# Two stacked experts behind attention: one d_ff group of the first out matrix by seven block products, and a new plan

## The chip, the core and the metric

One core of one Trainium2 chip runs the whole program as one launch. The metric is the device time in microseconds (us), as the median of several executions. The engines are TensorE (PE), VectorE (DVE), ScalarE (ACT), GpSimd (POOL) and SyncE (SP, which issues most DMAs). Each engine works through its own instructions in the order in which they stand in the program, and semaphores order the engines against each other.

## What is computed

```python
# attention: 4 batches, 12 heads, 448 tokens, head width 64; q and k are RMS-normed first
attn_out = softmax(scale * q_n @ k_n.T) @ v
x = attn_out.transpose(0, 2, 1, 3).reshape(1792, 768)
# first expert: d_model 768, d_ff 2048
h = x @ w_in
g = np.where(h > 0.0, h, np.exp(np.minimum(h, 0.0)) - 1.0)
x = g @ w_out
# second expert: d_ff 1536
xn = x / rms * rms_g
g = xn @ w_gate
out = (g * sigmoid(g) * (xn @ w_val)) @ w_out2
```

## The kernel before

Activations lie transposed: d_model or d_ff on the 128 partitions, the 448 tokens of one batch along the row. All products are fp32. An operand is split into a high part, rounded to the type that TensorE takes at full pace, and a low part, the remainder; a 128x128 weight tile times 448 columns is then three matmuls (`mm3`, line 1159: high·high, high·low, low·high). A split is a copy (`copy`, on DVE, ACT or POOL) and a subtraction (`tt`, on DVE or POOL).

The work runs in stages (`STAGES`, line 617): attention for batch 0 alone, then the first expert for batch 0, for batch 1, the second expert for batches 0 and 1, the first expert for batches 2 and 3, the second expert for batches 2 and 3. Attention for the later batches is spread between them. In the stages with two batches a block of 2x2 matrices is multiplied with seven products instead of eight (`quad`, line 1193): the weights enter as A11, A12, A22 and four combinations S1 to S4, the activations as B11, B21, B22 and four combinations T1 to T4 made by `combo` (line 1220). Each combination is split like any operand. In `combo` the first combination, `t1 = b12 - b11` (line 1233), has both inputs in SBUF; for the second product of an expert (`tx is GX`) it is written to a PSUM bank.

Batches 2 and 3 of the first expert ("stage 3" below, counting from 0) have d_ff in four groups of four tiles. Each group makes h by two `h_quad` calls (seven products each, 63 matmuls), and then adds its share of `g @ w_out` with `acc_units` (line 1341), eight plain products: 6 output tiles, 2 batches, 4 d_ff tiles, 3 matmuls, that is 144 matmuls. The last stage, the second expert for batches 2 and 3 ("stage 4"), has three groups, each four `quad`s for gate and value, two `combo`s over their results, and three `quad`s for the out matrix, all from weight blocks that were split earlier and stored in DRAM, and are loaded by DMAs on POOL's queue (`b_ahead`, line 682).

Weights arrive packed (`w_convert`), are kept as fp32 in DRAM (`kept`) where they are used again, and are split into a ring of four SBUF tiles (`r_w`), which gets a fifth when stage 3 begins (line 1558). Combinations of weights for stage 4 are made ahead of time by `job` (line 697) during stage 3.

No instruction is issued when the code above is run. Everything is recorded (`plan.add`), and `Plan` (line 33) lays the recorded operations onto the five engines by list scheduling with prices per operation: `forward` places operations by rank, `backward` makes new ranks from the result, and the best of several passes is kept. `issue` then emits the order; that is why all of it carries line 348. `Plan.add` marks an operation `shared` if none of its operands is in PSUM: such a DVE operation is priced as unable to run beside a GpSimd operation. At the start `issue` also fills PE's waits with idle matmuls on `small` into bank 130 (`idle`), whose number comes from planned start times.

## Time and profile before

| | |
|---|---|
| median of 3 runs | 1226.96 us (1224.61 to 1228.07) |
| the profiled execution: its own time | 1222.62 us |
| the profiled execution: span from first to last instruction | 1220.8 us |
| busy: PE, DVE, ACT, POOL | 99%, 75%, 58%, 68% of the span |
| mean granted TensorE clock | 0.997 of full speed |

The profile is one execution. The rows read from it name an engine, an operation, what it writes and reads (tile names without buffer numbers: `gbig`, `xs` and `late` are operands' halves, `w` split weights, `bank` PSUM), and in brackets the time for which the engine had been idle and what ended that. A tile called `late` is a buffer of the attention that is used again under another type.

### The profile page before, as it was taken

What the parts mean: (1) busy time and instruction counts of PE and PEld (TensorE: products, weight loads), DVE (VectorE), ACT (ScalarE), POOL (GpSimd) and SP (SyncE); (2) the same over time, 40 slices, a digit from 0 to 9 for tenths busy, and PEclk for the clock granted to TensorE, in tenths of its full rate; (3) what the DMA queues carried; (4) which work ended last, traced back from release to release, by engine and by line L of the source; (5) the groups of instructions that cost most, each with busy time, mean ns of one, the idle gap of its engine ahead of it and who ended that gap; (6) DMA issues with size and microseconds to landing.
All of it is one profiled execution on the core that took longest, in us unless ns stands there. A gap on an engine that the chain in (4) does not pass through costs nothing.

```text
span 1220.8 us, 18816 instructions
## 1 busy us (share of the span) xinstructions
PE 1204.1 (99%) x6296; PEld 1012.9 (83%) x6296; DVE 919.7 (75%) x1521; ACT 711.1 (58%) x1447; POOL 835.6 (68%) x721
## 2 busy tenths in 40 slices
PE   9899999999999999999999999999999999999998
PEld 7458777778777787778999999999999988988997
DVE  7777988899535579754799799947666799568678
ACT  6986877767665677765564564756444743221121
POOL 3467887888657485427897699866464978476573
PEclk9999999999999999999999999999999999999999
DMA  7677886885534458856599799756452275965766
GB/s 253 202 261 251 277 288 208 265 249 180 171 121 123 142 202 308 268 165 212 189 343 313 258 372 327 245 175 196 158 184 96 70 219 158 269 197 157 237 192 202
DMA packets 120164, 265.52 MB, mean 217 GB/s; under 512 B 15742, under 2 KB 59012, under 8 KB 120068
## 3 DMA queue, kind: packets, MB, share of 16 engines
q1 hardware_dynamic: 90260, 205.79, 50.1%
q0 software_dynamic: 21168, 49.55, 14.3%
q10 hardware_dynamic: 8640, 8.99, 2.9%
q8 instruction: 49, 0.80, 0.3%
q14 instruction: 47, 0.39, 0.1%
HBM read 183.11 MB, written 81.17 MB: 216 GB/s over the span
## 4 chain that ended last, share of the span: by engine, by line
PE 89%; DVE 7%; ACT 3%; issue 1%; ACTq 0%; DVEq 0%
PE bank L348 89%; DVE bank L348 2%; DVE tbig L348 1%; ACT p L348 1%; ACT tbig L348 1%; DVE gbig L348 0%; ACT pt L348 0%; DVE wc L348 0%; DVE wt L348 0%; DVE pt L348 0%; ACT tk L348 0%; DVE ybig L348 0%; DVE ss L348 0%; ACT ybig L348 0%; DVE pj L348 0%
## 5 line engine op out<-in xcount | busy, mean ns | idle before, releaser
L348 PE MATMUL bank<-xs,w 128*128 128x448 f32 x1731 | 401.3, 371 | 1.3 <-DVE late L348 0.8
L348 PE MATMUL bank<-gbig,w 128*128 128x448 f32 x1603 | 361.2, 370 | 0.2 <-DVE gbig L348 0.2
L348 PEld LDWEIGHTS bank<-xs,w 128*128 128x128 f32 x1731 | 317.7, 188 | 35.9 <-issue 8.5
L348 PEld LDWEIGHTS bank<-gbig,w 128*128 128x128 f32 x1603 | 296.5, 188 | 31.6 <-issue 6.6
L348 POOL TENSOR_TENSOR w<-wc,w 128x768 fp32r<-128x768 f32 (+1 forms) x106 | 195.4, 1846 | 51.9 <-ACT w L348 37.3
L348 PE MATMUL bank<-late,w 128*128 128x448 f32 x647 | 164.1, 367 | 2.7 <-ACT late L348 2.7
L348 DVE TENSOR_REDUCE bank<-bank 128x1 f32<-128x448 f32 x168 | 98.8, 624 | 53.7 <-PE bank L348 53.6
L348 PEld LDWEIGHTS bank<-late,w 128*128 128x128 f32 x647 | 121.8, 188 | 13.9 <-ACT late L348 3.5
L348 POOL TENSOR_SCALAR w<-wc 128x768 fp32r<-128x768 f32 (+1 forms) x50 | 46.1, 922 | 80.7 <-PE bank L348 71.8
L348 ACT ACTIVATE p<-bank,nm,rr 128x448 f32<-128x448 f32 x126 | 90.2, 720 | 18.4 <-DVE nm L348 16.2
L348 DVE SCALAR_TENSOR_TENSOR wc<-wc,wt 128x768 int32<-128x768 int32 x68 | 87.4, 1285 | 16.6 <-ACT wc L348 10.0
L348 ACT ACTIVATE tbig<-bank 128x448 f32<-128x448 f32 x85 | 46.0, 542 | 76.0 <-PE bank L348 54.5
L348 ACT ACTIVATE pt<-bank 128x384 f32<-128x384 f32 (+2 forms) x175 | 75.3, 451 | 24.2 <-PE bank L348 20.5
L348 ACT ACTIVATE w<-wc 128x768 fp32r<-128x768 f32 (+1 forms) x75 | 58.5, 782 | 42.7 <-PE bank L348 34.0
L348 DVE TENSOR_TENSOR ybig<-bank,ybig 128x448 f32<-128x448 f32 x72 | 44.4, 618 | 40.6 <-PE bank L348 40.3
L348 PE MATMUL bank<-ident,p 128*128 128x128 f32 x441 | 69.9, 277 | 2.3 <-ACT pt L348 2.2
L348 DVE TENSOR_TENSOR tbig<-bank,tbig 128x448 f32<-128x448 f32 x93 | 56.4, 618 | 20.6 <-PE bank L348 18.9
L348 DVE TENSOR_SCALAR wt<-wr 128x768 uint16<-128x768 uint16 x68 | 68.6, 1009 | 1.1 <-DMA wr<-wst 0.8
L348 PEld LDWEIGHTS bank<-ident,p 128*128 128x128 f32 x441 | 53.7, 141 | 17.5 <-ACT pt L348 5.4
L348 ACT ACTIVATE wt<-wr 128x768 uint16<-128x768 uint8 x50 | 54.4, 1089 | 22.7 <-DVE wc L348 12.2
L348 POOL TENSOR_TENSOR ql<-rw,qh 128x512 fp32r<-128x512 f32 x38 | 53.8, 1431 | 3.2 <-ACT qh L348 2.6
L348 PE MATMUL bank<-pt,rv 128*64 128x448 f32 x252 | 53.1, 550 | 1.0 <-ACT pt L348 1.0
(264 smaller groups left out, 2251.1 us busy)
## 6 DMA issues: line engine op xcount, KB each, us to landing
wr<-wst SPq DMA_DIRECT2D x68, 768.0 KB
wc<-kept SPq DMA_DIRECT2D x64, 384.0 KB
kept<-wc SPq DMA_DIRECT2D x52, 384.0 KB
w<-bgv_S POOLq DMA_DIRECT2D x38, 384.0 KB, 3.9
bgv_A<-w SPq DMA_DIRECT2D x36, 384.0 KB
bgv_S<-w SPq DMA_DIRECT2D x32, 384.0 KB
rw<-qk SPq DMA_DIRECT2D x21, 512.0 KB
w<-bgv_A POOLq DMA_DIRECT2D x28, 384.0 KB, 4.1
```

The costliest lines, as they stand in the source:

```text
L348: return lambda *a, **k: f(*[real(x) for x in a], **{n: real(x) for n, x in k.items()})
```

## The change

1. **Stage 3, group 1 by seven products.** The new function `fast_experts` takes the place of `first_experts` for batches 2 and 3. For d_ff group 1 (`SEVEN = (1,)`) the out matrix is no longer added by eight plain products but by three `quad`s, 3 x 7 x 2 x 3 = 126 matmuls for 144. The weights' blocks come from `w_out`, which reads them from `kept` and makes S1 to S4 with four `tt`; the activations' blocks come from a `combo` over the four h tiles of each `h_quad`. For this group the accumulators `ybig` go to DRAM (`parts`) and their space is lent to the operands; the sums of the group go through `parts` too, and are loaded back behind it.
2. **First halves ahead.** The first `h_quad` of a group now stands ahead of the out products of the group before it.
3. **Split out weights kept.** On their second use (batch 1) the split out weights of groups 0, 2 and 3 are stored in DRAM (`both`, 12 tiles of 768 KB), and stage 3 loads them by POOL's queue instead of splitting them.
4. **Blocks in pairs.** Stage 4's weight blocks are stored and loaded two to a DMA (`pairs`): 87 DMAs on POOL's queue in the whole program where there were 147. `job` makes gate and value blocks in halves.
5. **The fifth weight tile** joins only behind stage 3; its space holds h and partial sums during it.
6. **The plan.** Another seed, then 20 local changes of rank (`MOVES`); an operation with two inputs in SBUF and its output in PSUM now counts as `shared`; the number of idle matmuls comes from a second pass over the finished order (`times`).

```diff
-    PASSES = 12
-    SEED = 33
+    PASSES = 11
+    SEED = 47
+    MOVES = (
+        (645977, 260.9, 275.9, 8.0, 1, 0),
...
-        shared = port and not any(getattr(ap.tensor, "_space", None) == PSUM for ap in list(outs) + list(ins) if ap is not None)
+        banked = [getattr(ap.tensor, "_space", None) == PSUM for ap in list(outs) + list(ins) if ap is not None]
+        shared = port and not any(banked[len([o for o in outs if o is not None]):] if sum(not b for b in banked) > 1 else banked)
...
+        for seed, lo, hi, size, own, more in self.MOVES:
+            noise = random.Random(seed)
+            rank = list(best[1]) if own else self.backward(*best)
+            for i in range(n):
+                if lo <= best[1][i] < hi:
+                    rank[i] += size * (noise.random() - 0.5)
+            for _ in range(more):
+                rank = self.backward(*self.forward(rank))
+            best = self.forward(rank)
...
-        t, end = self.IDLE[0], self.start_t[self.first_use]
+        at = self.times(order, eng)
+        t, end = self.IDLE[0], at[self.first_use]
...
+    r_y = Ring(tiles=r_sq.t + [wr[0][:, k * S:(k + 1) * S] for k in range(2)])
...
+    r_h = Ring(tiles=[pt_own[0][:, k] for k in range(3)] + [wr[0][:, 2 * S:3 * S]])
...
+                res += ins(g, 1) + ins(g + 1, 0) if g else ins(0, 0) + ins(0, 1) + ins(1, 0)
+                if g in SEVEN:
+                    res += [("o", j, nums[k + nf], q) for q in range(3) for j in range(3)]
+                else:
+                    res += [("c", nums[k + nf + j]) for j in range(OG)]
...
+            if n in both:
+                w = spl_w[i] = r_w.next()
+                dma(w.rearrange("p a n -> p (a n)"), both[n].rearrange("p a n -> p (a n)"), P * WN * 8, by="g")
+                return
...
+    def w_out(i, j, n0, q):
+        n = 2 * P
+        if j == 0:
+            c, s0, s1 = r_wc.next(), r_ws.next(), r_ws.next()
+            a21 = s1[:, n:2 * n]
+            for x, v in ((a21, 4), (c[:, 2 * n:3 * n], 6), (c[:, 0:n], 0), (c[:, n:2 * n], 2)):
+                m, k = divmod(8 * q + v, CW)
+                dma(x, kept[n0 + m][:, k * P:k * P + n], P * n * 4)
...
+            tt(x1, a21, a22, ALU.add)
+            tt(x2, x1, a11, ALU.subtract)
+            tt(x3, a11, a21, ALU.subtract)
+            tt(s1[:, 0:n], a12, x2, ALU.subtract)
+            duo["o"] = (c, s0, s1[:, 0:n])
+        spl_w[i] = split_w(duo["o"][j], n if j == 2 else WN)
...
+    def spread_h(f, bs, hs, seven):
+        if not seven:
+            for (i, j), t in hs.items():
+                split_g((f + i, bs[j]), t)
+            return
+        combo(f // 2 % 2, [hs[i, j] for j in range(2) for i in range(2)], {}, GX, gslots, 2)
...
+            if first:
+                ahead = h_quad(f0, bs)
+                yield
+            spread_h(f0, bs, ahead, seven)
+            h = h_quad(f0 + 2, bs)
+            if last:
+                drop_combos()
+            spread_h(f0 + 2, bs, h, seven)
+            yield
+            if not last:
+                ahead = h_quad(f0 + NF1, bs)
+                yield
+            if not seven:
+                yield from acc_units(bs, f0, NF1, first, last, y, False, y_done)
+                continue
+            for k in range(3):
+                quad(out_eat(first, E_ORDER[2 * k:2 * k + 2]), tx=GX, take=take_out)
...
-                    r_w.grow([wide[0].rearrange("p (a n) -> p a n", a=2)])
                     combos(ahead[1])
...
+            r_w.grow([wide[0].rearrange("p (a n) -> p a n", a=2)])
             j = r_w.k % len(r_w.t)
-            r_b.t = [t.rearrange("p a n -> p (a n)")[:, h * WN:(h + 1) * WN] for t in r_w.t[j:] + r_w.t[:j] for h in range(2)]
+            r_b.t = [t.rearrange("p a n -> p (a n)") for t in r_w.t[j:] + r_w.t[:j]]
```

PE's queue at the start of the program, before and then after. The rows on `small` are the idle matmuls; `ident,rsb` makes the gain of the norms, `ident,rr` spreads the first norm factors that k waits for, `qh` and `ql` are the first scores.

```order
L348 MATMUL bank_130<-small 128x128 x28
L348 MATMUL bank_133<-ident,rsb_125 128x1
L348 MATMUL bank_130<-small 128x128 x20
L348 MATMUL bank_134<-ident,rr_114 64x128 x8
L348 MATMUL bank_130<-small 128x128 x3
L348 MATMUL bank_134<-ident,rr_114 64x128 x8
L348 MATMUL bank_130<-small 128x128 x3
L348 MATMUL bank_127<-qh 128x448
```

```order
L445 MATMUL bank_130<-small 128x128 x35
L445 MATMUL bank_133<-ident,rsb_125 128x1
L445 MATMUL bank_130<-small 128x128 x6
L445 MATMUL bank_134<-ident,rr_114 64x128 x8
L445 MATMUL bank_130<-small 128x128 x3
L445 MATMUL bank_134<-ident,rr_114 64x128 x8
L445 MATMUL bank_130<-small 128x128 x3
L445 MATMUL bank_127<-qh 128x448
```

Seven idle matmuls moved ahead of the gain, and fourteen of the twenty behind it are gone.

ACT's queue during the attention of batch 0, before and then after. `pe` and `pt` are copies of transposed probabilities out of the banks 131 to 133, which PE's next transposes write; `tk` squares tokens for a later norm; `p` and `tbig` with `sm` are exponentials.

```order
L348 ACTIVATE p_106,sm_117<-bank_127,nm_119,rr_114 128x448
L348 ACTIVATE pe_110<-bank_131 64x64 x2
L348 ACTIVATE tk_99<-tk_99 128x960
L348 ACTIVATE pt_107<-bank_131 128x3x64
L348 ACTIVATE pt_108<-bank_131 128x3x64
L348 ACTIVATE ybig<-bank_133 128x384
```

```order
L445 ACTIVATE pe_110<-bank_131 64x64 x2
L445 ACTIVATE pt_108<-bank_131 128x3x64
L445 ACTIVATE pt_107<-bank_131 128x3x64
L445 ACTIVATE p_106,sm_117<-bank_130,nm_119,rr_114 128x448
L445 ACTIVATE ybig<-bank_133 128x384
L445 ACTIVATE ybig<-bank_132 128x384
L445 ACTIVATE p_106,sm_117<-bank_127,nm_119,rr_114 128x448
L445 ACTIVATE pt_107<-bank_131 128x384
L445 ACTIVATE ybig<-bank_132 128x384
L445 ACTIVATE ybig<-bank_133 128x384
L445 ACTIVATE tk_99<-tk_99 128x960
```

The squaring of `tk` moved from between the copies out of bank 131 to behind them.

DVE's queue in stage 4, at the second group's second `combo`, before and then after. `pj` and `pt` hold gate times value; the row `bank_132<-pj_109,pt_107` (after: `bank_133<-pj_109,pt_107`) is `t1`. Each row that writes `pt` or `pj` completes a block, whose split by ACT and POOL can start then.

```order
L348 TENSOR_TENSOR bank_130<-tbig,bank_130 128x448
L348 TENSOR_TENSOR bank_131<-bank_131,rsb_124 128x448
L348 TENSOR_TENSOR pt_107<-pt_107,bank_130 128x448
L348 TENSOR_TENSOR pj_109<-pj_109,bank_131 128x448
L348 TENSOR_TENSOR bank_132<-pj_109,pt_107 128x448
L348 TENSOR_TENSOR bank_133<-pt_107,bank_132 128x448
```

```order
L445 TENSOR_TENSOR pt_107<-pt_107,bank_127 128x448
L445 TENSOR_TENSOR tbig<-bank_130,tbig 128x448
L445 TENSOR_TENSOR rsb_124<-bank_130,tbig 128x448
L445 TENSOR_TENSOR bank_132<-bank_132,tbig 128x448
L445 TENSOR_TENSOR pj_109<-pj_109,bank_132 128x448
L445 TENSOR_TENSOR bank_133<-pj_109,pt_107 128x448
L445 TENSOR_TENSOR bank_131<-tbig,bank_131 128x448
L445 TENSOR_TENSOR bank_134<-pt_107,bank_133 128x448
L445 TENSOR_TENSOR pt_107<-pt_107,bank_131 128x448
```

Before, a block `pt` is completed two rows ahead of `t1`; after, one is completed five rows ahead of it, and another only three rows behind it.

## Rows read from the trace of the kernel before

**Rows 1.** The page's first part: busy time, share, instructions of each engine.

```profile
PE 1204.1 (99%) x6296; PEld 1012.9 (83%) x6296; DVE 919.7 (75%) x1521; ACT 711.1 (58%) x1447; POOL 835.6 (68%) x721
```

**Rows 2.** Busy time by stretch: its length, engines with counts, clock, DMA share, GB/s.

```profile
600.00:1000.00 400.00, 400.00 (x1966) 368.69 (x1965) 316.01 (x477) 226.34 (x404) 293.26 (x224) 1.00 0.68 227
...
765.00:985.00 220.00, 220.00 (x1085) 203.40 (x1084) 153.35 (x269) 131.11 (x263) 146.89 (x118) 1.00 0.49 156
...
1100.00:1221.00 121.00, 113.13 (x542) 102.28 (x540) 91.55 (x145) 20.59 (x39) 69.03 (x94) 0.98 0.69 197
```

**Rows 3.** PE's waits from 980 us on: for whom, total, times, longest.

```profile
PE bank L348 <- ACT late L348: 2.7, 2, 1.9
PE bank L348 <- DVE late L348: 0.8, 1, 0.8
PE bank L348 <- DVE gbig L348: 0.6, 2, 0.5
PE bank L348 <- DVE tbig L348: 0.6, 1, 0.6
```

**Rows 4.** Timeline at the start, PE and DVE: start, length, engine, operation.

```profile
9.22 0.38 PE L348 MATMUL bank<-ident,rsb 1*128 1x1 f32 x2
9.52 4.73 PE L348 MATMUL bank<-small 128*128 128x128 f32 x40
...
11.92 0.30 DVE L348 SCALAR_TENSOR_TENSOR rr<-bank,rr 128x30 f32<-128x30 f32 x2
...
14.18 1.09 PE L348 MATMUL bank<-ident,rr 128*64 128x128 f32 x16
```

**Rows 5.** Timeline of ACT and PE around PE's longest wait in attention.

```profile
45.85 1.00 ACT L348 ACTIVATE tk<-tk 128x960 f32<-128x960 f32 x1
46.76 0.53 ACT L348 ACTIVATE pt<-bank 128x192 f32<-128x192 f32 x2
...
47.35 0.55 PE L348 MATMUL bank<-ident,p 128*128 128x128 f32 x3 [1.63 <-ACT pt L348]
```

**Rows 6.** Busy time in the two stretches at a lower clock.

```profile
49.20:52.60 3.40, 3.40 (x14) 1.62 (x13) 2.67 (x6) 3.31 (x9) 1.70 (x2) 0.51 0.40 138
...
1114.20:1117.50 3.30, 3.27 (x9) 2.58 (x9) 2.06 (x4) 1.15 (x3) 1.31 (x2) 0.50 0.09 7
```

**Rows 7.** DVE's groups by shape in stage 4: count, busy us, mean ns.

```profile
L348 DVE TENSOR_TENSOR bank<-pj,pt 128x448 f32<-128x448 f32 x6 | 11.2, 1862 | 0.1
...
L348 DVE TENSOR_TENSOR bank<-pt,bank 128x448 f32<-128x448 f32 x6 | 3.8, 630 | 1.2 <-ACT late L348 0.7
```

**Rows 8.** Timeline of POOL, DVE and PE around PE's longest wait in stage 4.

```profile
1109.49 3.10 DVE L348 TENSOR_TENSOR bank<-pj,pt 128x448 f32<-128x448 f32 x1
...
1109.82 1.16 POOL L348 TENSOR_TENSOR gbig<-pt,late 128x448 fp32r<-128x448 f32 x1
1110.94 1.15 POOL L348 TENSOR_TENSOR late<-pt,gbig 128x448 fp32r<-128x448 f32 x1
...
1112.70 0.63 DVE L348 TENSOR_TENSOR bank<-pt,bank 128x448 f32<-128x448 f32 x1
...
1113.95 0.63 PE L348 MATMUL bank<-late,w 128*128 128x448 f32 x1 [1.88 <-ACT late L348]
```

**Rows 9.** Timeline of PE at the other two of these waits.

```profile
1089.03 2.70 PE L348 MATMUL bank<-xs,w 128*128 128x448 f32 x12 [0.85 <-DVE late L348]
...
1194.69 0.47 PE L348 MATMUL bank<-late,w 128*128 128x448 f32 x1 [0.83 <-ACT late L348]
1195.35 0.47 PE L348 MATMUL bank<-gbig,w 128*128 128x448 f32 x1 [0.19 <-DVE gbig L348]
```

**Rows 10.** The page's costliest groups: a weight's split, a sum, a copy.

```profile
L348 POOL TENSOR_TENSOR w<-wc,w 128x768 fp32r<-128x768 f32 (+1 forms) x106 | 195.4, 1846 | 51.9 <-ACT w L348 37.3
...
L348 ACT ACTIVATE w<-wc 128x768 fp32r<-128x768 f32 (+1 forms) x75 | 58.5, 782 | 42.7 <-PE bank L348 34.0
...
L348 DVE TENSOR_TENSOR tbig<-bank,tbig 128x448 f32<-128x448 f32 x93 | 56.4, 618 | 20.6 <-PE bank L348 18.9
```

## What the change will do to the time

> **What bounds the kernel now.** The page's first part comes first: PE is busy for 1204.1 of 1220.8 us, every other engine for 75% or less [rows 1]. So time leaves this kernel in two ways only: PE gets less to do, or PE waits less. The view by stretches says how dense "busy" is: from 600 to 1000 us PE has no idle time and 1966 matmuls in 400 us, one in 0.2035 us, at full clock [rows 2]. Nearly all of them have 448 columns, so this is the price of one such matmul, and no other engine's work shows there at all. From 765 to 985 us, about where stage 3 lies, it is the same, with DVE at 153, ACT at 131 and POOL at 147 of 220 us [rows 2].
>
> PE's idle time lies at the two ends. The view of waits from 980 us on gives 2.7 us for ACT's `late`, 0.8 for DVE's `late`, 0.6 and 0.6 [rows 3]. In attention one wait is the longest, 1.63 us at 47.35 us [rows 5]. Two of these waits cost more than their length: just behind the 1.63 us at 47.35 and the 1.88 us at 1113.95 the granted clock is half, for 3.4 and 3.3 us [rows 5, 6, 8], the level of 1.2 GHz instead of 2.4; half of that time is lost, 1.7 and 1.65 us. The waits of 0.85 and 0.83 us [rows 9] have no such stretch behind them.
>
> **Part 1, seven products for eight.** The order holds 18 fewer matmuls of 448 columns, 126 for 144 in one out group. All lie in a stage without idle time, so they come off whole: 18 x 0.2035 = **3.7 us** [rows 2]. What the group adds is not on PE. Two `combo`s split 14 operands where 8 were split, and combine with 8 `tt`; three `quad`s add 36 `tt` where 12 were needed: about 6 copies and 38 `tt`. At 0.62 us for a sum [rows 10] and as much for a copy that is some 27 us, spread over DVE, ACT and POOL. Part 3 takes back 12 splits of out weights, 12 x (0.78 + 1.85) = 31 us [rows 10]. Stage 3 has 67 us of idle DVE, 89 of ACT and 73 of POOL [rows 2], so the balance is free. The sums' way through DRAM and the larger loads are SP's and POOL's issues; the DMA engines are busy for 0.49 of this stage [rows 2], and what hides them is the `h_quad` that now stands ahead of each out group, 63 matmuls or 12.8 us. I take 0. If that cover fails, the price is the slower rival below.
>
> **Part 2, the start.** PE spends 9.52 to 14.25 us on 20 idle matmuls (40 records, 0.237 us each) and spreads the first norm factors at 14.18, though DVE had finished them by 11.92 + 0.30 = 12.2 us [rows 4]. So the idle matmuls themselves are late by 2 us, and everything in attention's first scores hangs on that. In the new order seven more stand ahead of the gain and fourteen fewer behind it: the gain moves from 9.22 to 9.22 + 7 x 0.237 = 10.9, six more idle ones and the gain's own 0.3 us end at 12.6, and the spread starts there instead of at 14.18. That is 1.6 us. The load that the gain needs has moved four places back in SP's queue; if it arrives only later than 10.9 us, this eats into it. I take **1.5 us**, between 0 and 1.6.
>
> **Part 3, stage 4's waits.** The rows of DVE by shape show what delays PE: `t1` (`bank<-pj,pt`) takes 1862 ns on average, its neighbour of the same shape with one input in PSUM 630 [rows 7]. The worst one takes 3.10 us, from 1109.49 on, and inside it POOL runs two subtractions of operands in SBUF back to back, 1.16 and 1.15 us; `t1` ends 0.5 us behind the second, ACT's copies follow, and PE gets its operand at 1113.95 [rows 8]. So a DVE instruction with two inputs in SBUF stands still while POOL works, wherever its output goes. The old plan priced it as free of that, since its output is in PSUM. The new plan prices it right, and the order shows it: before, a block was completed two rows ahead of `t1`, and its split went to POOL just then; after, that block is completed three rows behind `t1`, and `t1` meets the one split of the block five rows ahead, with about 3 us to run off first. The third group's `t1` has the same order.
>
> What hangs on it: 0.85, 1.88, 0.83 and 0.19 us of waits [rows 8, 9] and 1.65 us of clock [rows 6], 5.4 us in all. At the mean length of its neighbour `t1` would be 2.48 us shorter in the second group, more than the 1.88 us that PE waits. But then DVE itself is next: between the last product that `t1` needs and the first matmul that waits behind it stand 24 matmuls (4.9 us) in the second and 21 (4.3 us) in the third group, for some six DVE instructions of 0.62 us, 3.7 us and the hops. So not much is left over, and some waits will stay. I take **3.5 us**; the bounds are 0 and 5.4. The two waits of 0.6 and 0.45 us where stage 4 begins [rows 3] hang on the norm and I leave them.
>
> **Part 4, attention's waits.** At 47.35 PE waits for two copies that stand behind the 1.00 us squaring of `tk` on ACT [rows 5]. The new order puts that squaring behind all copies of that round. That would give back up to 1.63 + 1.7 = 3.3 us [rows 5, 6]. But all of attention is reordered, ACT is tight there, and a new wait of the same kind anywhere costs the same 3.3 us. Bounds are -3.3 and 3.3; I take **1.5 us**, since this one place is plainly better.
>
> **The pairs of blocks** keep the bytes and halve the issues on POOL's queue; five buffers of two blocks hold as much as ten of one. I take 0.
>
> **Sum.** 3.7 + 1.5 + 3.5 + 1.5 = 10.2 us. The profiled execution, 1222.62 us with 1.8 us around its span, would become 1212.4 us. The median of the runs stands 4.3 us above that execution, so the median becomes 1226.96 - 10.2 = **1216.8 us**.
>
> **Rivals.** *Only the count.* The plan is new everywhere, and it can have as many waits as the old one, elsewhere. Then the 18 matmuls alone remain: 1223.3 us, a gain of 3.7 us or 0.30%, which is just what a measurement of this kernel can tell from no change. For it: every wait of before is a place where the plan's prices were off, and most prices stayed. Against it: the start's 1.5 us is in the order, and the price that was off in stage 4 is the one that was mended.
>
> *The port moves into stage 3.* The two new `combo`s of the seven group hold two more `t1`. If each is held as the one at 1109.49 was, PE waits 1.88 us and loses 1.65 to the clock, 7.1 us for two; with nothing gained in stage 4 and attention that is 1226.96 - 3.7 - 1.5 + 7.1 = 1228.9 us. The Trainium skill's page "SBUF — State Buffer" (section "Who interferes with whom") says so for any such pair: a VectorE instruction with two SBUF inputs contends with a GpSimd instruction that reads SBUF, and whichever issued first blocks the other for its whole length. By that rule the group's added SBUF-to-SBUF work speaks against this change; the trace agrees as far as the 3.10 us over two POOL instructions go. Against the rival: the first of these `t1` has an `h_quad` of other work around it, and the plan prices both.
>
> *Slower: weights run dry in stage 3.* The ring has four tiles there instead of five. In the new order 21 matmuls (4.3 us) stand at the tightest six places between the last use of a weight tile and the first use of its next content, where the four-tile ring of stage 2 had 27 (5.5 us) and ran without idle time. The refill takes 0.78 + 1.85 = 2.6 us [rows 10] if ACT and POOL start at once. POOL has one queue: if one 1.85 us split stands ahead there, 4.5 us pass and PE waits 0.2; if two stand ahead, 2.0 us and the clock's 1.65. Six such waits are 22 us: 1226.96 - 10.2 + 22 = 1239 us. It decides from four of them on (14.6 us), where the time passes the old one by over 0.3%. Against it: POOL idles a third of that stage [rows 2], and splits of other weights are fewer than before.
>
> That the change doesn't do what it says can be left out: the order has the 18 matmuls less.
>
> **How the numbers follow.** Forecast 72%, only the count 15%, port 7%, dry weights 6%. The forecast's own bounds: with all of parts 2 to 4, 3.7 + 1.6 + 5.4 + 3.3 = 14.0 us, 1213.0 us; with parts 3 and 4 at nothing and the start's 1.5, 1221.8 us. The lower end gets the 1.7 us by which the runs of before scatter, 1211.3; the upper end takes in half of "only the count", 1223.6. Faster by over 0.3%: the forecast and 6 points of "only the count", 78%. Within 0.3%: 9 and 7, 16%. Slower: 6%.
>
> **What would show it.** 18 fewer matmul instructions of 448 columns between the start of stage 3 and its end, and no idle time in it; `ident,rr` on PE near 12.6 us; `bank<-pj,pt` near 0.6 to 1.2 us on average instead of 1.86; no stretch of half clock in stage 4, and waits of PE behind 980 us under 2.5 us in all instead of 4.7. The prediction is wrong if stage 3 shows PE waits for `w`, or if a new wait over 1.6 us brings back a stretch at half clock in attention.

## The result and the profile after

The changed kernel takes 1214.55 us (median of 6 runs, 1213.05 to 1217.1), the kernel before 1226.07 us beside it (6 runs, 1224.61 to 1228.07): a ratio of 0.991 with an interval of 0.9899 to 0.992, 11.5 us less by the medians. The forecast was 1216.8 us. The profiled execution of after takes 1213.99 us with a span of 1212.0, against 1222.62 and 1220.8 of before, so the two traces show 8.8 of the 11.5 us. The rest lies between executions: the profiled one of before was 3.5 us faster than its median here, that of after 0.6.

Busy time and the page's first line after the change, beside [rows 1], and busy time by stretch beside [rows 2] (length, then PE, PE's weight loads, DVE, ACT, POOL with counts, granted clock, DMA share, GB/s):

```profile
PE 1196.5 (99%) x6262; PEld 1005.5 (83%) x6262; DVE 932.9 (77%) x1559; ACT 715.4 (59%) x1482; POOL 824.7 (68%) x686
...
755.00:975.00 220.00, 220.00 (x1080) 202.43 (x1079) 169.36 (x316) 136.21 (x292) 163.71 (x144) 1.00 0.73 238
```

PE is as full as before. Stage 3 has no idle PE time up to 975 us, though its DMA share has risen from 0.49 to 0.73. PE gets 1080 matmuls into these 220 us where 1085 stand in [rows 2], which is 1.0 us at the same length; the part on two paces below has more on that. What changed is best seen from three marks on PE that both traces hold: the norm of batch 1 (`gbig,ones` at 467.52 us before), the last norm ahead of stage 4's first products (986.70), and the last matmul. The same three marks in each trace, before and then after:

```profile
467.52 0.65 PE L348 MATMUL bank<-gbig,ones 128*128 128x448 f32 x2
...
986.70 0.57 PE L348 MATMUL bank<-gbig,ones 128*128 128x448 f32 x2
...
1215.71 0.36 PE L348 MATMUL bank<-gbig,w 128*128 128x448 f32 x1
```

```profile
464.53 0.65 PE L445 MATMUL bank<-gbig,ones 128*128 128x448 f32 x2
...
986.48 0.57 PE L445 MATMUL bank<-gbig,ones 128*128 128x448 f32 x2
...
1206.92 0.36 PE L445 MATMUL bank<-gbig,w 128*128 128x448 f32 x1
```

| stretch | before | after | difference |
|---|---|---|---|
| start to the norm of batch 1 | 467.5 us | 464.5 us | -3.0 us |
| from there to the last norm | 519.2 | 522.0 | +2.8 |
| from there to the last matmul | 229.0 | 220.4 | -8.6 |

The last stretch holds 1080 matmuls of 448 columns in both traces, so its 8.6 us are waits, clock and pace alone. The middle one holds 21 of them fewer (three of the 21 moved ahead of the first mark) and 12 small ones more, about 3.0 us of work less, and still takes 2.8 us longer. So the gain did not come where the matmuls were taken out. The split hangs a little on the mark: with the norm of batch 2 (983.82 before, 981.75 after) in place of the last norm the two differences are +0.9 and -6.7 us, since a wait of 1.53 us after the change lies between the two norms.

PE's waits from 975 us on, after, beside [rows 3] (for whom, total, times, longest):

```profile
PE bank L445 <- DVE late L445: 1.5, 1, 1.5
PE bank L445 <- DMA w<-pair: 0.4, 1, 0.4
```

1.9 us where there were 4.7. The first of them, at 984.73 us, lies ahead of the last norm; behind it 0.4 us are left, and no stretch of half clock.

DVE's groups by shape in stage 4, beside [rows 7], and two single `t1` from DVE's timeline, the second `combo`s of the second and third group:

```profile
L445 DVE TENSOR_TENSOR bank<-pj,pt 128x448 f32<-128x448 f32 x6 | 8.0, 1338 | 0.2
...
1103.75 0.63 DVE L445 TENSOR_TENSOR bank<-pj,pt 128x448 f32<-128x448 f32 x1
...
1180.72 0.65 DVE L445 TENSOR_TENSOR bank<-pj,pt 128x448 f32<-128x448 f32 x1
```

The `t1` that took 3.10 us at 1109.49 [rows 8] takes 0.63. The mean is 1338 and not 630 ns, because GpSimd still holds others: one at 1006.93 us takes 2.05, one at 1158.52 us 2.71.

The start, beside [rows 4] (timeline of DVE before, then of PE, POOL and DVE after):

```profile
7.87 0.22 DVE L348 TENSOR_SCALAR ones<-ident 128x128 fp32r<-128x128 f32 x1
...
9.16 1.26 POOL L445 TENSOR_TENSOR ql<-rw,qh 128x512 fp32r<-128x512 f32 x1 [8.71 <-ACT qh L445]
9.29 0.17 DVE L445 SCALAR_TENSOR_TENSOR bank<-bank,rr 128x15 f32<-128x15 f32 x1
9.37 1.14 DVE L445 TENSOR_SCALAR ones<-ident 128x128 fp32r<-128x128 f32 x1
10.39 0.44 POOL L445 TENSOR_TENSOR rsb<-rsb 1x128 f32<-1x128 f32 x1
10.43 0.18 DVE L445 TENSOR_SCALAR bank<-ss 128x30 f32<-128x30 f32 x1
...
13.12 1.09 PE L445 MATMUL bank<-ident,rr 128*64 128x128 f32 x16 [0.32 <-DVE rr L445]
```

The spread of the norm factors starts at 13.12 us instead of 14.18, not at 12.6. The idle matmuls end at 12.80, and PE then waits 0.32 us for DVE: DVE's `ones` takes 1.14 us, from 9.37 to 10.51, and the chain that makes `rr` goes on only then. Before, the same instruction took 0.22 us, with POOL idle. Now a subtraction on POOL runs from 9.16 to 10.42, and `ones` ends 0.09 us behind it. In the runs "old price" and "what is left of t1" below, `ones` takes 1.12 and 0.78 us and ends 0.08 and 0.09 us behind the same POOL instruction. So POOL held up a DVE instruction that has only one input in SBUF, too.

Around [rows 5] the wait of 1.63 us is gone, and the two stretches at half clock of [rows 6] have no counterpart in this trace: the first window is at full clock, with 19 matmuls where there were 14.

```profile
49.20:52.60 3.40, 3.40 (x19) 1.66 (x17) 3.22 (x8) 3.40 (x11) 0.96 (x2) 1.00 0.69 218
```

### The profile page after: what moved, and what is told of

Its sections match the earlier page's. It is cut to its first block, busy times and chain, and to the rows that moved or that the text cites. A ratio compares the mean times of both kernels' runs of the same rounds, so it can differ in the third digit from the quotient of the medians.

```text
span 1212.0 us, 18931 instructions
## 1 busy us (share of the span) xinstructions
PE 1196.5 (99%) x6262; PEld 1005.5 (83%) x6262; DVE 932.9 (77%) x1559; ACT 715.4 (59%) x1482; POOL 824.7 (68%) x686
## 4 chain that ended last, share of the span: by engine, by line
PE 87%; DVE 5%; ACT 4%; issue 2%; DMA 1%; POOL 0%; ACTq 0%; DVEq 0%; POOLq 0%
PE bank L445 87%; DVE bank L445 1%; ACT tbig L445 1%; DMA w<-pair 1%; DVE wc L445 1%; ACT p L445 1%; DVE ss L445 1%; DVE late L445 1%; DMA pair<-late 1%; DVE last L445 0%; ACT pt L445 0%; DVE tbig L445 0%; DVE xs L445 0%; DMA tk<-tok 0%; DVE wt L445 0%
## 5 line engine op out<-in xcount | busy, mean ns | idle before, releaser
L445 PE MATMUL bank<-gbig,w 128*128 128x448 f32 x1675 | 377.3, 370 | 0.4 <-DMA w<-pair 0.4
L445 PEld LDWEIGHTS bank<-gbig,w 128*128 128x128 f32 x1675 | 309.1, 188 | 32.6 <-issue 6.1
L445 POOL TENSOR_TENSOR w<-wc,w 128x768 fp32r<-128x768 f32 (+1 forms) x100 | 184.4, 1845 | 62.0 <-ACT w L445 57.8
L445 PE MATMUL bank<-late,w 128*128 128x448 f32 x740 | 185.8, 366 | 0.1
L445 PEld LDWEIGHTS bank<-late,w 128*128 128x128 f32 x740 | 138.8, 188 | 12.0 <-DVE late L445 0.4
L445 ACT ACTIVATE pt<-bank 128x384 f32<-128x384 f32 (+2 forms) x191 | 85.4, 459 | 43.5 <-PE bank L445 34.9
L445 DVE TENSOR_SCALAR wt<-wr 128x768 uint16<-128x768 uint16 x68 | 73.4, 1080 | 2.1 <-DMA wr<-wst 1.9
L445 POOL TENSOR_TENSOR w<-p,w 128x768 fp32r<-128x768 f32 (+1 forms) x33 | 62.1, 1886 | 18.5 <-ACT w L445 18.2
L445 POOL DMA_DIRECT2D w<-pair x60 | 33.5, 558 | 55.5 <-PE bank L445 54.4
L445 ACT ACTIVATE tbig<-bank 128x448 f32<-128x448 f32 x69 | 37.1, 540 | 53.1 <-PE bank L445 45.9
L445 POOL TENSOR_SCALAR w<-wc 128x768 fp32r<-128x768 f32 (+1 forms) x39 | 33.3, 854 | 48.7 <-PE bank L445 45.6
```

The costliest lines, as they stand in the source:

```text
L445: return lambda *a, **k: f(*[real(x) for x in a], **{n: real(x) for n, x in k.items()})
```

## Experiments

Gains are ratios to the runs of the kernel before beside them, turned into us at 1226; the interval stands in brackets. (By the difference of the medians the 18 matmuls and the `t1` edit come to 2.6 and 7.1 us instead of 1.5 and 7.8; later expectations use those figures.) "Its own order" means that an edit changed no place of any other instruction.

### 18 matmuls less in the order of before

In group 1's out products the third matmul of `mm3` is not issued in 18 places:

```diff
-            for o, l, r, start, stop in mms:
+            for o, l, r, start, stop in mms[:-1] if drop else mms:
```

> The kernel before, in its own order, with 18 matmuls of 448 columns left out in group 1's out products of stage 3 (low times high of two d_ff tiles in 9 of 12 products), so this part of the sum is incomplete. Both theories (the parts add up; only the count matters) expect 18 x 0.2035 = 3.7 us less: PE has no idle time there, and no other engine's work is changed. If the time falls by under 2 us, something behind stage 3 takes it back.

Measured: 1223.51 us, ratio 0.9988, a gain of 1.5 us [-1.1, 4.0]. In the trace the middle stretch shrinks by 1.4 us (519.2 to 517.8), not 3.7. PE now meets a wait that was not there, and runs slower elsewhere; all of the loss lies ahead of 975 us, none at the hand-over to stage 4. A wait in stage 3, and one 20 us stretch (same columns as above):

```profile
844.63 1.21 PE L348 MATMUL bank<-gbig,late 128*128 128x448 f32 x4 [0.32 <-DVE gbig L348]
...
780.00:800.00 20.00, 20.00 (x98) 18.16 (x98) 13.90 (x25) 13.79 (x28) 16.39 (x13) 1.00 0.74 255
```

98 matmuls in 20 us are one in 0.206 us; more on that below. The interval holds the 3.7 us that both theories expected, and it holds nothing as well. The wait at 47.57 us was 1.63 us again, with the clock at full behind it.

### 72 matmuls less

The same in all four groups:

```diff
-    ... (1, 2) if not half and f0 == NF1 and (b == 2 or b == 3 and e < 3) else ()
+    ... (1, 2) if not half and b >= 2 and (b == 2 or e < 3) else ()
```

> The kernel before in its own order, with 18 high-by-low matmuls left out of the out products of each of the four d_ff groups of stage 3, 72 in all instead of the 18 of the first run (the sums are wrong in value by that part). Theory A (stage 3 has no idle PE time, so a matmul left out is worth its 0.2035 us): 72 x 0.2035 = 14.7 us, 1211.4 us, and the stretch from attention's last pv to stage 4's norms shrinks by as much, 425.7 to 411.0 us, with no PE waits in it. Theory B (the first run's 2.6 us for 18 is the true price, since something else stands close behind PE there): about 10 us, 1216 us, with waits of PE for w, gbig or late between 600 and 980 us.

Measured: 1218.39 us, ratio 0.9926, a gain of 9.1 us [6.0, 12.1]; the middle stretch shrinks by 8.9 us for 14.7 us of matmuls, so 5.8 us are lost. It is theory B's size, but with waits for other tiles. Matched matmul by matmul with before, 2.4 us are lost up to 968 us, where PE has only 0.5 us of idle time, and 3.3 us behind that, where stage 3 ends. There the rows show 2.7 us of idle time; the two largest waits, and what DVE, POOL and ACT did ahead of the first:

```profile
964.69 3.47 DVE L348 TENSOR_TENSOR late<-tbig,late 128x448 fp32r<-128x448 f32 x1
...
966.51 1.15 POOL L348 TENSOR_TENSOR ybig<-ybig 128x448 f32<-128x448 f32 x1
...
968.79 0.58 ACT L348 ACTIVATE tbig<-ybig 128x448 f32<-128x448 f32 x1 [2.10 <-DVE ybig L348]
...
970.40 0.86 PE L348 MATMUL bank<-late,w 128*128 128x448 f32 x3 [1.48 <-ACT ybig L348]
974.33 0.67 PE L348 MATMUL bank<-xs,w 128*128 128x448 f32 x2 [1.02 <-POOL xs L348]
```

PE arrives earlier at the hand-over to the second expert and stands there behind the chain on DVE, ACT and POOL, which had kept up only because PE was slower. The head of that chain is a DVE instruction with two inputs in SBUF that takes 3.47 us while POOL runs three instructions; it took 3.49 us before as well (at 967.59), and held up nobody on PE. So time taken from a full PE is not whole when another engine stands close behind: 5.8 of 14.7 us were lost.

### t1 with one input in PSUM

In stage 4 and the other `combo`s over gate times value, `t1` reads its own PSUM bank in place of the SBUF tile b11 (so it is no longer b12 - b11; its place and shape are the same):

```diff
-        tt(t1, b12, b11, ALU.subtract)
+        V.tensor_tensor(out=t1, in0=b12, in1=t1, op=ALU.subtract)   # where tx is GX
```

> The kernel before, in its own order; in stage 4 the first combination t1 reads its second input from its own PSUM bank instead of SBUF, so that its value is not b12 - b11. Theory A (the shared port delays t1, and t1 delays PE): t1 takes 0.63 us instead of 1.86 in all six places, PE's waits of 0.85, 1.88, 0.83 and 0.19 us go and so does the half clock behind the second, 5.4 us less. Theory B (DVE's own chain is next and keeps PE waiting): t1 takes 0.63 us, but half of the waits stay, 2 to 3 us less. Theory C (only the count matters, waits move on): within 1 us of before.

Measured: 1219.02 us, ratio 0.9936, a gain of 7.8 us [5.4, 10.4]. DVE by shape and PE's waits from 975 us on:

```profile
L348 DVE TENSOR_TENSOR bank<-pj,bank 128x448 f32<-128x448 f32 x6 | 3.7, 624 | 0.1
...
PE bank L348 <- DVE tbig L348: 0.5, 1, 0.5
PE bank L348 <- DVE gbig L348: 0.3, 1, 0.3
```

624 ns instead of 1862, 0.8 us of waits instead of 4.7, no half clock: so `t1` beside GpSimd alone makes the four waits that the prediction listed and the half clock behind them. The two waits of 0.61 and 0.45 us at the start of the stage are still there, 0.50 and 0.33 us long. From the last norm to the last matmul it is 222.2 us for 229.0, a gain of 6.8, where the rows account for 3.9 us of waits and 1.65 of half clock, 5.6 in all. The Trainium skill, page "SBUF — State Buffer", section "Who interferes with whom", states that a VectorE instruction with two SBUF inputs contends with a GpSimd instruction that reads SBUF, and that one with at most one SBUF input does not, outside the 2-port perf modes. These runs agree, at 1862 and 624 ns for the same shape.

### What is left of t1 in the changed kernel

The same edit on the changed kernel, in its own order.

> The changed kernel in its own order, and t1 of the combos over gate times value (stage 4 and the second expert of batches 0 and 1, and the group by seven products in stage 3) reads its PSUM bank as second input in place of the SBUF tile b11, so these combinations are wrong in value; count, shape and place of the instructions stay. Theory A (port: what is left of t1 in the changed kernel still holds PE): t1 falls from 1338 to about 630 ns, the waits behind 975 us from 1.9 to under 1, and 1 to 2 us more are won: about 1213 us. Theory B (the new order has taken t1 off PE's path): t1 falls all the same, the waits stay at about 1.9 us, and the time is within 0.1% of the changed kernel, 1214.5 us.

Measured: 1215.1 us, ratio 0.9915 [0.9899, 0.9932], no different from the changed kernel's 0.991. `t1` takes 625 ns, and the one wait behind 975 us is still the 1.5 us for `late`. Theory B: the 2.71 us at 1158.52 hold nobody up.

### Fewer idle matmuls at the start

12 instead of 20 behind the gain, in the order of before:

```diff
+        counts = [28, 12, 3, 3, 7]
```

> The kernel before, in its own order, with 12 instead of 20 idle matmuls behind the gain at the start. Theory A (attention hangs on the first scores): the spread of the first norm factors starts at 9.52 + 12 x 0.237 = 12.4 us instead of 14.18, the first scores 1.8 us earlier, and the end 1.8 us earlier. Theory B (ACT paces attention and takes it back): the first scores come 1.8 us earlier, PE waits that much longer in the next 40 us, and the time stays within 0.5 us.

Measured: 1223.54 us, ratio 0.998, a gain of 2.5 us [0.2, 4.7]. In the trace the first scores come at 16.06 us instead of 17.84, but the norm of batch 0 comes no earlier. Here is where PE stands instead (timeline of ACT, its DMA issues and PE):

```profile
258.07 1.11 ACTq L352 DMA_DIRECT2D rb<-scr  x2
259.27 0.44 ACTq L352 DMA_DIRECT2D rsum<-rt  x1
259.76 0.49 ACT L352 ACTIVATE pt<-bank 128x384 f32<-128x384 f32 x1 [3.54 <-DMA kept<-wc]
...
260.31 0.55 PE L352 MATMUL bank<-ident,p 128*128 128x128 f32 x3 [2.26 <-ACT pt L352]
...
260.80:264.10 3.30, 3.30 (x11) 2.83 (x10) 2.62 (x4) 2.84 (x8) 1.44 (x2) 0.50 0.73 237
```

Before, the same matmul started at 260.57 us after 0.34 us of waiting. PE came earlier, but `pt` stands on ACT behind DMA issues that went out hardly earlier (`rb` at 258.07 for 258.34 us), and half clock followed. So in this execution the start's gain was given back at 260 us; that the median still gained says that it is not so in each.

### The squaring ahead of the pt copies

ACT's squaring at 45.85 us [rows 5] works on 64 of 960 columns, and DVE takes a maximum behind it in place of the sum:

```diff
-                "a": (c_a(n), lambda: A.activation(out=tk, in_=tk, func=AF.Square)),
+                ... out=tk[:, 0:D] if i == 8 else tk, in_=tk[:, 0:D] if i == 8 else tk ...
```

> The kernel before, in its own order; the one squaring of tokens that stands ahead of the copies out of bank 131 near 45.85 us squares 64 of 960 columns, and its sums are replaced by a maximum, so one pair's norm is wrong. Theory A (this place makes the wait and the wait makes the half clock): the squaring falls from 1.00 to about 0.15 us, the wait at 47.35 from 1.63 to about 0.8, no half clock behind it, 2.5 us less. Theory B (another wait follows at once): the half clock or a wait of the same size appears within 10 us, less than 1 us gained.

Measured: 1224.76 us, ratio 0.9989, a gain of 1.3 us [-0.6, 3.3], not to be told from none. The 24th product with v comes 1.9 us earlier (53.0 for 54.9 us), and there is no half clock. That clock is worth 1.7 of the 1.9 us, and it is not the edit's alone: in the run with 18 matmuls less the unchanged wait of 1.63 us had full clock behind it. And then:

```profile
101.21 1.01 ACT L348 ACTIVATE tk<-tk 128x960 f32<-128x960 f32 x1 [4.90 <-DMA tk<-tok]
...
104.65 3.92 PE L348 MATMUL bank<-xs,w 128*128 128x448 f32 x18 [1.59 <-DVE tbig L348]
```

ACT reaches a later squaring earlier than its tokens and stands still for 4.90 us, with all that is queued behind it. The edit need not be the cause: with attention as before, ACT stands there for 1.36 us in the trace of before, but for 4.12 us in that of `t1` and 3.45 in that of the 72 matmuls, with waits of PE behind it there too.

### The four edits together

Count, t1, idle matmuls and squaring, edited as in the single runs, in the order of before.

> The kernel before in its own order, with the four single edits of this study together: 18 high-by-low matmuls left out of group 1's out products, t1 of the combos over gate times value reading its own PSUM bank, 12 instead of 20 idle matmuls behind the gain, and the squaring of tk ahead of the pt copies on 64 of 960 columns with a maximum in place of the sum (outputs are wrong in value). By their profiles the edits are worth 3.7 us (count), 6.8 to 7.1 us (t1), 1.8 us where the first scores begin, and 1.9 us at the 24th pv product of batch 0; alone they measured 2.6, 7.1, 2.5 and 1.3 us, each with 2 us of uncertainty. Theory A (they add up): 1226.1 - 13.5 = 1212.6 us or less. Theory B (what is won ahead of 260 us is taken back where ACT stands on its DMAs at 104 to 115 and 260 us; only count and t1 remain): 1226.1 - 10.8 = 1215.3 us, the norms of batch 0 at 275 to 277 us as before, not at 272.

Measured: 1213.55 us, ratio 0.99, a gain of 12.3 us [9.4, 15.0], as large as the change's. The interval holds both theories. In the trace batch 0's norm comes at 275.9 us (275.6 before), as theory B said, the middle stretch gains 1.5 us, the last one 7.9. But the gain of the start was not lost where B put it alone. PE waits only 0.38 us at 260 us, and 1.3 us at 109 and 113; another 3.4 us go to a stretch at half clock near 24 us, where before lost 1.7 at 49:

```profile
24.40:31.20 6.80, 6.77 (x27) 4.56 (x27) 4.39 (x16) 5.44 (x16) 3.91 (x5) 0.50 0.47 152
```

So the four edits together are as large as the change, but not made of the same parts: the change gains 3.0 us ahead of the norm of batch 1 and loses 2.8 in the middle.

### Old price, new plan

The changed kernel with the planner's old rule for `shared`, planned anew.

```diff
-        shared = port and not any(banked[len([o for o in outs if o is not None]):] if sum(not b for b in banked) > 1 else banked)
+        shared = port and not any(banked)
```

> The changed kernel, but the planner counts an operation as held by GpSimd only if none of its operands is in PSUM, as before the change; the same seed, the same local changes of rank, re-planned. In the order t1 of stage 4's second group's second combo stands one row ahead of the block pt that it used to stand behind, so nearly as in the changed kernel; other places are shuffled. Theory A (the mended price is what took t1 out of GpSimd's way): t1 goes back to 1.6 to 2.0 us on average (1862 ns before, 1338 after), PE's waits behind 975 us to 4 us or more (1.9 after) with a stretch of half clock, and the time to about 1219 to 1221 us. Theory B (the new arrangement of the stage does it, whatever the price): t1 stays at 1.2 to 1.5 us, the waits behind 975 us near 2, the time 1213 to 1217 us.

Measured: 1245.54 us, ratio 1.0169 [1.0146, 1.0193]. Both theories missed the time. In stage 4 it is theory B: `t1` there and PE's waits from 1020 us on are

```profile
L445 DVE TENSOR_TENSOR bank<-pj,pt 128x448 f32<-128x448 f32 x6 | 8.4, 1403 | 0.1
...
PE bank L445 <- DVE gbig L445: 0.7, 1, 0.7
PE bank L445 <- DVE late L445: 0.5, 1, 0.5
```

and from the last norm to the last matmul it takes 221.1 us, nearly as the changed kernel's 220.4. So the mended price is not what gives stage 4 its order, which is nearly the changed kernel's. What was lost lies ahead of it: 25.3 us of PE waits behind the first 15 us (8.6 in the changed kernel) and some 10 us by half clock.

### No group, or two groups, by seven products

First by the changed kernel's seed and rank changes, planned anew:

```diff
-SEVEN = (1,)
+SEVEN = ()        # and, in another run, SEVEN = (1, 2)
```

> The changed kernel with no d_ff group by seven products: all four groups' out products by eight blocks, 18 matmuls more, everything else of the change kept, re-planned with the same seed and the same local changes of rank. Theory A (PE has no idle time in stage 3, so matmuls count whole): 18 x 0.2035 = 3.7 us longer than the changed kernel from the norm of the second expert back to the start, with no idle PE from 600 to 980 us; but the shuffled order loses what the start and stage 4 had by luck of the plan, so about 1218 to 1222 us. Theory B (the group brings waits of its own, by its operands and its sums through DRAM, which eat part of the 18 matmuls; from 600 to 1000 us the changed kernel's matmuls lie 2.7 us further apart than those of before): without the group these 2.7 us vanish as well, so the stretch from attention's last pv to the norms of stage 4 grows by only about 1 us against the changed kernel, and the time stays at 1214 to 1217 us.

> The changed kernel with two d_ff groups of the four (1 and 2) by seven products: 18 matmuls less again, re-planned with the same seed and the same local changes of rank. Theory A (matmuls count whole, and the group brings no waits): 3.7 us less than the changed kernel, about 1211 us, if the shuffled order loses nothing at the ends. Theory B (every group by seven products costs waits of 1 to 3 us through its operands, and two of them next to each other more, since the accumulators go through DRAM twice): PE shows waits between 700 and 980 us, and the time is 1214 to 1220 us.

Measured: 1259.53 us (1.0282 [1.0257, 1.0307]) without the group, 1247.41 us (1.0183 [1.016, 1.0206]) with two. No theory had that. PE waits 33 and 29.2 us behind the first 15, and loses about 12 us more to half clock in each. The twenty rank changes were found for one list of instructions and do not carry over to another.

Then with a seed and rank changes searched for the very program:

> The changed kernel with no d_ff group by seven products, as in the earlier run without it, but now with a seed and local changes of rank searched for this very program (1 of 60 seeds, then 20 accepted changes), as the changed kernel's own were for it. So this differs from the changed kernel by the group of seven, at a like quality of plan. Theory A (the group is worth its 18 matmuls and no more): 18 x 0.2035 = 3.7 us slower than the changed kernel, 1217 to 1220 us. Theory B (the group's operands and its sums through DRAM cost PE time elsewhere): within 1.5 us of the changed kernel, 1213 to 1216 us. Either way far below the 1259.5 us of the run that kept the changed kernel's seed and rank changes, if those were what spoilt it.

> The changed kernel with the d_ff groups 0 and 1 by seven products, 18 matmuls less again, with a seed and 30 local changes of rank searched for this program. Theory A (with a plan of its own each group is worth 18 x 0.2035 = 3.7 us): 3.7 us less than the changed kernel, 1210 to 1212 us. Theory B (two such groups next to each other run out of time for their operands, or the start, where 19 idle matmuls stand behind the gain again, loses what the count wins): 1213 to 1217 us, with PE waits between 570 and 980 us, or the first scores at 18 us or later instead of 16.8.

Measured: 1229.32 us (1.0033 [1.0021, 1.0045]) without a group, 1229.87 us (1.0034 [1.002, 1.0047]) with groups 0 and 1. So a plan of its own took 30 us off the version without a group (groups 0 and 1 had no earlier run), and still both are slower than the kernel before; 36 matmuls of difference, 7.3 us, do not show between them. With two groups PE waits 19.7 us behind the first 15, among them for weights in stage 3, the second time with half clock behind it:

```profile
802.20 1.69 PE L455 MATMUL bank<-gbig,w 128*128 128x448 f32 x7 [0.77 <-DVE w L455]
...
905.13 0.47 PE L455 MATMUL bank<-late,w 128*128 128x448 f32 x1 [1.94 <-DVE w L455]
...
905.00:908.40 3.40, 2.68 (x7) 2.18 (x8) 3.40 (x9) 2.06 (x5) 1.33 (x2) 0.64 0.35 117
```

What the group is worth at an equal plan stays open: plans of the same making lie further apart on the chip than 3.7 us. The marks say as much as one trace each can: without a group the stretch up to the norm of batch 1 is 8.0 us longer than in the changed kernel, though no product of the group stands there, with 12 matmuls of 448 columns less. From there to the end it is 4.9 us longer for 30 matmuls more (6.1 us). So where the group acts the difference is near the count, as theory A said, and the plan lost its time elsewhere. None of these versions beats the changed kernel. What the kept weights, the pairs of blocks and the halves ahead are worth by themselves no run shows.

## Why the prediction was right, and which of its terms were not

The total was 2.3 us off, within its range, and the gain 1.3 us (11.5 for 10.2). Its parts were off by more and made up for one another, so that the total came this close is luck. The traces also hold only 8.8 of the 11.5 us. Of the signs that it named, PE's waits behind 980 us (under 2.5) and the full clock in stage 4 came true; `t1` takes 1.34 us on average, not 0.6 to 1.2, and the spread starts at 13.12 us, not 12.6.

**Part 1, the count (3.7 us).** The matmuls are gone and stage 3 has no idle time up to 975 us, as forecast. That they "come off whole" failed as a step: the middle stretch is 2.8 us longer with 3.0 us less work in it, so 5.8 us were lost there. Four waits hold 3.9 of them by their rows and 4.5 by the starts of matmuls; 0.5 more went to the slower of the two paces described below, and the rest is not placed. The four in PE's timeline after, and what DVE and POOL did ahead of the last:

```profile
467.30 0.88 PE L445 MATMUL bank<-xs,w 128*128 128x448 f32 x3 [0.84 <-ACT tbig L445]
470.62 0.55 PE L445 MATMUL bank<-ident,p 128*128 128x128 f32 x3 [0.89 <-ACT pt L445]
...
639.08 0.86 PE L445 MATMUL bank<-qh,w 128*128 128x448 f32 x3 [0.68 <-DVE pj L445]
...
981.93 1.17 POOL L445 TENSOR_TENSOR xs<-xf,xs 128x448 fp32r<-128x448 f32 x1
982.51 2.16 DVE L445 TENSOR_TENSOR late<-tbig,late 128x448 fp32r<-128x448 f32 x1
983.06 1.12 POOL L445 TENSOR_TENSOR xs<-last,xs 128x448 fp32r<-128x448 f32 x1
...
984.60 0.61 DVE L445 TENSOR_TENSOR gbig<-tbig,gbig 128x448 fp32r<-128x448 f32 x1
984.73 0.68 PE L445 MATMUL bank<-late,late 128*128 128x448 f32 x2 [1.53 <-DVE late L445]
```

None of them lies in the group of seven, whose `combo`s stand at 815 and 841 us. Three lie ahead of stage 3, so they come with the new order and not from the count. The one at 984.73 is the hand-over to stage 4, the place at which the run with 72 matmuls less lost most of its time too. It has the same cause as stage 4's waits of before, as far as rows can show it: a DVE instruction with two inputs in SBUF takes 2.16 us over two POOL instructions and ends 0.49 us behind the second, where its like, started while POOL is free, takes 0.61. No run took POOL away there. The prediction looked at the idle time of the stage that loses the work, and not at the waits that a new order brings elsewhere, nor at the place where PE next waits for others.

**Part 2, the start (1.5 us): 1.06.** The right mechanism, and the gain came at 10.89 us as forecast; but DVE's chain, with `ones` held by POOL in it, became the next limit, 0.32 us behind the idle matmuls' end at 12.80. That the start's gain lasts is shown only by the median of the single run (0.2 to 4.7 us); its trace gave it back at 260 us.

**Part 3, stage 4 (3.5 us, bounds 0 and 5.4): 8.6.** The mechanism was right: `t1` beside GpSimd, and with t1 alone edited the time fell by 7.8 us and the stretch by 6.8. The size was not, for three reasons. First, the rows of idle time leave part of each wait out: a matmul's row lasts 0.36 us while the next one starts 0.20 us behind it, so the shown end of the last one runs into the wait. Counted by starts, the six waits behind the last norm cost 5.9 us where their rows have 4.8; after the change 0.5 us are left. Second, the waits of 0.61 and 0.45 us that the prediction left to the norm are gone too. Third, the argument that DVE would be "next" was too careful: none of the listed waits stayed, and the 0.4 us left are for a pair of weight blocks. With 1.9 us of half clock and 0.8 us less at the slower pace that makes about 8 of the 8.6 us.

The reason given, the mended price, fell with the old-price run, which has nearly the same order there. The order itself, read row by row, was the sound evidence. And the prediction's remark that the trace agrees with "whichever issued first blocks the other" goes too far: in [rows 8] `t1` starts 0.33 us ahead of the first POOL instruction and is held for both, and so it is, with 3.08 to 3.10 us, in the four other traces with that `t1` unchanged. How the two engines take turns, these rows do not settle.

The Trainium skill's page "Perfetto Trace Analysis", section "Identifying the Most-Contended Engine", warns that TensorE's busy share is not a good measure of how close a kernel is to the roofline, because pipelined matmuls look smaller in the trace. Here PE is at 99% in both traces, with 8.6 us between equal work, so the share told nothing of that difference.

**Part 4, attention (1.5 us, bounds 3.3 either way).** The wait at 47.35 and its half clock are gone, and by the norm of batch 1 the changed kernel is 3.0 us ahead, 1.06 of it from the start. Of the other 1.9 us the half clock alone is 1.7, and that stretch stands only in some executions. Behind that come the two new waits of 0.84 and 0.89 us above. Of the single edit's 1.9 us in batch 0 nothing measurable stayed. The term was near in size in this pair of traces; how much of it lasts the runs don't settle.

**The rivals.** *Only the count* named the wrong remainder, for the count was given back. But its premise, as many waits elsewhere, was half right: by the rows PE waits 10.1 us in all where it waited 11.7, 4.5 us less behind the last norm and 3.9 more in the middle stretch. *The port in stage 3*: the two `t1` of the group take 814 ns on average (1.6 us in all), and no half clock follows. The same hold-up came back one step further on, at the hand-over, with 1.53 us. *Weights run dry*: not in the changed kernel, which has no wait for `w` but 0.4 us for `w<-pair` in stage 4; but with two groups and another plan it is there, 0.77 and 1.94 us. So the rival was real, and the plan that was on hand avoided it.

## What to carry to other kernels

Compare equal work between the same marks of two traces before adding up rows of idle time: it shows what the waits cost in full, and where a saving is given back. When PE gets less to do, look for the next place at which it meets another engine; with 72 matmuls less 5.8 of 14.7 us were lost, 3.3 of them there. When a DVE instruction takes three times as long as its like, look at what POOL ran beside it. And where a recorded plan sets the order, judge that order, not its rules: for the same program the plan with one price put back took 1245.5 us instead of 1214.6, though its stage 4 was nearly as good.

## What the hardware showed that was not expected

**Two paces of the same matmul at full clock.** By the intervals between starts, back-to-back matmuls of 448 columns run at 202.7 ns or, for 4 to 42 us at a time, at 206.7 ns. Two stretches of before without idle time (same columns as above), 101 and 98 matmuls in 20 us:

```profile
600.00:620.00 20.00, 20.00 (x101) 18.51 (x100) 16.27 (x23) 10.95 (x17) 16.76 (x12) 1.00 0.72 256
660.00:680.00 20.00, 20.00 (x98) 18.16 (x97) 15.25 (x18) 7.23 (x9) 12.68 (x10) 1.00 0.77 257
```

Many of them keep their place with the order: the one from 642 to 684 us stands in before and in every run with its order, some us later where the start came later. With 18 matmuls left out two more long ones appeared, 775 to 816 and 936 to 975 us, in both traces without these matmuls; the first of these two runs lost 1.0 us more to the slower pace than before did in the middle stretch, part of what it was short of. But the order alone does not set them: between 780 and 940 us the changed kernel has long ones at 881 to 894 and 900 to 936 us, and its run with t1 edited at 788 to 827 and 841 to 883 instead. What starts and ends them stays open; in the two rows above, DMA share (0.72 and 0.77) and the other engines' load differ little.

**Half clock does not always follow a wait.** The changed kernel and the run on it with t1 edited have the same order, and PE waits 1.19 us for `p` near 23 us in both. Behind it the clock is full (2.4 GHz) in the first, and half (1.2 GHz) in the second:

```profile
24.50:28.00 3.50, 2.98 (x20) 1.79 (x20) 3.46 (x12) 3.46 (x13) 0.58 (x1) 1.00 0.65 210
```

```profile
24.50:28.00 3.50, 3.48 (x14) 2.49 (x16) 3.17 (x12) 3.02 (x10) 0.99 (x2) 0.52 0.54 160
```

The wait of 1.88 us at 1113.95 had half clock behind it in the traces of before, of the 18 matmuls, the idle matmuls and the squaring (1.87 to 1.88 us each), but not in that of the 72 matmuls (1.95 us). The wait of 1.63 us in attention had it in three traces, those of before, of t1 and of the 72 matmuls, and not in those of the 18 matmuls and the idle matmuls. So the 1.7 us that the prediction put on each of these stretches are the price of some executions, and one profile doesn't tell of how many.
